# Loading weight chunks up to three ahead of their decoding, in the first batch of a fused attention, convolution-gate and token-mixing kernel

## The chip, the core and the metric

The kernel runs on one core of one Trainium2 chip. The metric is the device time of one execution in microseconds (us). Engines are named as in the profile: PE is TensorE (PEld its weight loads), DVE is VectorE, ACT is ScalarE, POOL is GpSimd, SP is SyncE. SP does nothing here but issue all transfers from one queue, in one order.

## The reference, cut to what matters

```python
# attention with 4 sink keys and a window of 128, batch 2, 8 heads, 768 tokens, head size 64
scores = scale * (q @ k.T);  scores = where(is_sink | in_window, scores, -1e9)
a = exp(scores - max);  a = a / (sum(a) + 1e-9);  x = a @ v          # -> [2, 768, 512]
# gate: w_in [512, 1024], conv_w [3, 1024], w_out [1024, 512]
h = relu(x @ w_in);  c = depthwise conv of h over 3 tokens;  x = (h * sigmoid(c)) @ w_out
# token mixing
theta = x @ w_theta;  y = w_tok_r @ (x * cos(theta)) + w_tok_i @ (x * sin(theta))
u = x + y;  out = u + relu(u @ w_ch)
```

The weights arrive as 64-bit floats.

## The kernel before, in words

A matmul of the gate is three matmuls: each operand is held as a high and a low part (`mm3`, L122 to L124). Since a weight arrives as 64-bit words, it is read in chunks of 128 rows by 512 words (512 KB) into one of six slots of 4 KB per partition and **decoded** there: ACT scales the high words (L98), DVE does three integer steps (L99 to L101), ACT writes the high part (L80), DVE the low part (L82), and the slot is free again. `w_in` and `w_out` are sixteen such chunks, numbered 0 to 15: 0 to 3 are the first half of `w_in`, 4 to 7 the first half of `w_out`, 8 to 11 and 12 to 15 the second halves. Chunks 0 and 1 are loaded ahead of everything, in before and after alike.

Attention runs in four **units** (two batches, two halves of three query tiles), each of four head **pairs**. A pair loads q and k (L261, L262) into one of three buffers, makes scores on PE (L272), their maximum on DVE (L288), the exponential on ACT (L292), sums and reciprocals on DVE (L295, L296), and normalised probabilities split into two fp16 parts by ACT (L314) and DVE (L315) in a buffer `pb`, which SP transposes by DMA into `pt` (L322). The first four heads are transposed by PE instead (L339 to L343). The values of a pair of a batch are read into a slot (L198), scaled and split by ACT and DVE into a second slot (L203 to L210), and transposed by DMA into `vp` (L212). PE forms the sink rows from `vp` (L235) and multiplies `pt` by `vp` (L380); ACT and DVE store the result as `xg` (L400, L401). So **weights and values draw on the same six slots**, taken in the order of a free list.

The gate runs in blocks: scores of the hidden layer from all four pairs' `xg` (L122 to L124 into `ps_h`), relu and convolution on ACT and DVE (L597 to L606), then L616 to L622. The sixteen blocks of the first four groups of 256 tokens are written between the pairs of the units; after each pair of unit n the code also decodes CHUNKS[n][p] chunks: 1, 1, 3, 6 in the first unit, 2, 2, 0, 1 in the second. The remaining blocks, the rotations and the token mixing follow after the attention.

What an engine does in which order is not what the code's order says: a list scheduler reorders each engine's instructions and SP's transfers when the program is built. Moving an allocation in the code therefore moves the slots that later loads get, their dependences, and through them the order on every engine.

Before the change a chunk's load is written at the place where it is decoded in the first batch; only in the third unit, where no chunk is left, stands a 1.

Of the kernel before, what the change touches and what calls it, by code (L numbers as in the profile page):

```python
# [50 lines left out]
DEC2 = 3  # L51
SA = 2
EARLY = 1
W_AHEAD = (0, 0, 1, 0)
BIG = 8.0e9
SP = 4096.0
TWO_PI = 2.0 * math.pi
# [485 lines left out]
def weight_load(tc, c, i):  # L543

    n, i = divmod(i, 8)
    if i < CC:
        src = c.w_in[i * P : (i + 1) * P, 2 * n * DM : 2 * (n + 1) * DM]
    else:
        src = c.w_out[(4 * n + i - CC) * P : (4 * n + i - CC + 1) * P, :]
    raw, slot = c.raw.tile([P, DM, 2], I32)  # L550
    tc.nc.sync.dma_start(raw.rearrange("p n w -> p (n w)"), src)
    return raw, slot
# [171 lines left out]
def body(tc, c, general):  # L724
# [49 lines left out]
    for n, unit in enumerate(units):  # L774
        unit.start()
        for p in range(4):
            unit.pair(p)
            for _ in range(CHUNKS[n][p]):
                next(weights)
                while len(c.wraw) < W_AHEAD[n] and c.nw + len(c.wraw) < 16:  # L780
                    c.wraw.append(weight_load(tc, c, c.nw + len(c.wraw)))
# [167 lines left out]
```

## Time and profile before

| what | us |
|---|---|
| median of 3 runs | 461.32 |
| the runs | 460.97, 461.32, 463.22 |
| the profiled execution, whole | 463.23 |
| its span, first to last instruction | 461.4 |
| PE busy in the span | 413.2 (90%) |
| DVE busy | 334.2 (72%) |
| ACT busy | 291.5 (63%) |
| POOL busy | 35.5 (8%) |

The span is what the rows of a trace add up to; 1.8 us of the execution lie around it. Busy shares are means over stages with different limits, so the windows of the span, not the totals, tell which engine is full at what time. The bracket behind a row of a timeline is the time that the engine stood idle just before that instruction and the instruction or transfer that ended it.

### The profile page before, as it was taken

How to read it: one execution, taken by the hardware profiler on the slowest of the kernel's cores; microseconds unless marked ns; L12 is line 12 of the kernel's file. 1: busy time of each engine (PE TensorE's matmuls, PEld its weight loads, DVE VectorE, ACT ScalarE, POOL GpSimd, SP SyncE). 2: the span in 40 equal slices, each digit the busy share in tenths (PEclk: the TensorE clock that was granted, in tenths of full speed). 3: DMA queues.
4: the chain of work that ended last, by engine and by line, in shares of the span. 5: the costliest groups of instructions: out<-in, count | busy, mean ns of one | idle time of the engine just before them, and what ended most of it. 6: DMA issues, size and time to landing. Idle time of an engine off the chain costs nothing.

```text
span 461.4 us, 7204 instructions
## 1 busy us (share of the span) xinstructions
PE 413.2 (90%) x2376; PEld 334.9 (73%) x2376; DVE 334.2 (72%) x898; ACT 291.5 (63%) x717; POOL 35.5 (8%) x120
## 2 busy tenths in 40 slices
PE   1587739699889999999999999899979999999995
PEld 0465528587677887988888887688858888888874
DVE  3879989999889886865699877995599963211132
ACT  2799878978899886875685778875675431100010
POOL 4001210031221110110000000000000000000000
PEclk9989867899999999999999999999999999999999
DMA  6786999459888442212435200230037620000012
GB/s 180 208 230 148 248 247 293 107 117 201 181 169 166 103 92 48 47 38 39 139 88 164 70 1 0 70 92 23 0 93 223 195 84 23 24 23 24 23 45 75
DMA packets 73245, 50.07 MB, mean 109 GB/s; under 512 B 59376, under 2 KB 62448, under 8 KB 73200
## 3 DMA queue, kind: packets, MB, share of 16 engines
q1 hardware_dynamic: 73200, 49.54, 42.6%
q8 instruction: 20, 0.33, 0.3%
q14 instruction: 25, 0.20, 0.1%
HBM read 32.09 MB, written 3.15 MB: 76 GB/s over the span
## 4 chain that ended last, share of the span: by engine, by line
PE 67%; DVE 16%; DMA 8%; ACT 4%; issue 3%; SPq 1%; POOL 0%; DVEq 0%; ACTq 0%; POOLq 0%
PE ps_y L123 7%; PE ps_y L124 7%; PE ps_y L122 7%; PE ps_x L616 5%; PE ps_s L272 5%; PE ps_x L617 4%; PE ps_m L122 4%; PE ps_x L622 4%; PE ps_m L124 4%; PE ps_m L123 4%; PE ps_o L380 4%; PE ps_h L122 4%; PE ps_h L124 3%; PE ps_h L123 3%; DMA pt<-pb 3%
## 5 line engine op out<-in xcount | busy, mean ns | idle before, releaser
L272 PE MATMUL ps_s<-qk 128*128 128x260 f32 (+1 forms) x192 | 60.4, 420 | 20.4 <-DVE mx L288 11.1
L122 PE MATMUL ps_y<-z_hi,wt_hi 128*128 128x512 f32 x144 | 57.7, 401 | 1.6 <-ACT z_hi L80 1.6
L122 PE MATMUL ps_h<-xg_hi,win_hi 128*128 128x258 f32 x192 | 58.6, 307 | 0.4 <-ACT h L597 0.4
L124 PE MATMUL ps_y<-z_lo,wt_hi 128*128 128x512 f32 x144 | 56.7, 397 | 0.4 <-DVE z_lo L82 0.4
L123 PE MATMUL ps_y<-z_hi,wt_lo 128*128 128x512 f32 x144 | 56.9, 395 | 0.0
L124 PE MATMUL ps_h<-xg_lo,win_hi 128*128 128x258 f32 x192 | 56.0, 296 | 0.4 <-DVE xg_lo L401 0.3
L272 PEld LDWEIGHTS ps_s<-qk 128*128 128x128 f32 x192 | 34.2, 211 | 29.5 <-DVE mx L288 15.6
L123 PE MATMUL ps_h<-xg_hi,win_lo 128*128 128x258 f32 x192 | 55.4, 290 | 0.0
L80 ACT ACTIVATE xt_hi<-ps_t 128x512 fp32r<-128x512 f32 x24 | 14.0, 594 | 61.1 <-PE ps_t L650 61.0
L292 ACT ACTIVATE e<-e,mx 128x260 f32<-128x260 f32 (+1 forms) x96 | 47.3, 496 | 7.2 <-DVE mx L288 6.9
L601 DVE SCALAR_TENSOR_TENSOR cv<-h,cw_t,cv 128x256 f32<-128x256 f32 x96 | 44.8, 478 | 6.8 <-ACT cv L599 6.1
L288 DVE CUSTOM_DVE_ANT_0 e<-ps_s,m 128x260 f32<-128x260 f32 (+1 forms) x96 | 37.7, 399 | 10.4 <-PE ps_s L272 9.0
L616 PE MATMUL ps_x<-wout_hi,ghi 128*128 128x512 f32 x96 | 40.9, 426 | 3.4 <-ACT ghi L80 3.4
L718 DVE SCALAR_TENSOR_TENSOR slot<-ps_m,slot 128x512 f32<-128x512 f32 x12 | 8.3, 691 | 44.1 <-PE ps_m L124 44.1
L122 PEld LDWEIGHTS ps_h<-xg_hi,win_hi 128*128 128x128 f32 x192 | 36.8, 192 | 3.7 <-ACT h L597 1.2
L617 PE MATMUL ps_x<-wout_lo,ghi 128*128 128x512 f32 x96 | 38.7, 403 | 0.0
L124 PEld LDWEIGHTS ps_h<-xg_lo,win_hi 128*128 128x128 f32 x192 | 36.8, 193 | 1.9 <-issue 0.5
L123 PEld LDWEIGHTS ps_h<-xg_hi,win_lo 128*128 128x128 f32 x192 | 36.9, 192 | 1.4
L314 ACT ACTIVATE pb<-e,ri 128x256 f16<-128x256 f32 (+1 forms) x84 | 35.4, 494 | 1.9 <-DVE ri L296 1.2
L315 DVE SCALAR_TENSOR_TENSOR pb<-e,ri,pb 128x256 f16<-128x256 f32 (+1 forms) x84 | 35.5, 459 | 1.2 <-ACT pb L314 1.1
L380 PE MATMUL ps_o<-pt,vp 128*64 128x256 f16 (+2 forms) x348 | 23.8, 261 | 11.8 <-DMA pt<-pb 5.4
L380 PEld LDWEIGHTS <-vp 128*64 128x64 f16 (+1 forms) x348 | 17.9, 113 | 22.5 <-issue 13.3
(134 smaller groups left out, 927.6 us busy)
## 6 DMA issues: line engine op xcount, KB each, us to landing
raw<-in_w_tok_r_dram SPq DMA_DIRECT2D x12, 384.0 KB, 3.3
raw<-in_w_tok_i_dram SPq DMA_DIRECT2D x12, 384.0 KB, 3.5
slot<-in_w_in_dram SPq DMA_DIRECT2D x8, 512.0 KB, 6.1
slot<-in_w_out_dram SPq DMA_DIRECT2D x8, 512.0 KB, 4.7
qk<-in_q_dram SPq DMA_DIRECT2D x32, 96.0 KB, 3.3
slot<-in_vt_dram SPq DMA_DIRECT2D x8, 384.0 KB, 3.7
out_dram<-slot SPq DMA_DIRECT2D x12, 256.0 KB, 2.0
qk<-in_k_dram SPq DMA_DIRECT2D x8, 262.0 KB, 3.2
```

The lines of the kernel that those rows point to most:

```text
L122: nc.tensor.matmul(out, whi, xhi, start=first, stop=False)
L123: nc.tensor.matmul(out, wlo, xhi, start=False, stop=False)
L124: nc.tensor.matmul(out, whi, xlo, start=False, stop=last)
L272: nc.tensor.matmul(ps[:, :n], qk[0][:, a, i * P : (i + 1) * P], qk[1][:, o : o + n], start=True, stop=True)
L288: nc.vector.tensor_tensor_reduce(out=e[:, i, :n], in0=ps[:, :n], in1=m, scale=-1.0 / math.sqrt(D), scalar=3.0e38, op0=ALU.add, op1=ALU.min ...
L292: nc.scalar.activation(e[:, i, :n], e[:, i, :n], AF.Exp, bias=mx[:, i : i + 1], scale=-1.0, accum_out=sm[:, i : i + 1])
L314: nc.scalar.activation(hi, src, AF.Copy, scale=r)
L315: nc.vector.scalar_tensor_tensor(lo, src, r, hi, ALU.mult, ALU.subtract)
L380: nc.tensor.matmul(po[a * D : (a + 1) * D, q], w[:, a * D : (a + 1) * D], pts[a][: w.shape[0], b0:b1, :], start=(n == 0), stop=(n == len(j ...
L601: nc.vector.scalar_tensor_tensor(cv[:, n, :], h[:, n, k : GT + k], w[:, k : k + 1], cv[:, n, :], ALU.mult, ALU.add)
L616: nc.tensor.matmul(self.px[t], ghi[:, n, s], whi, start=f2 == 0 and n == 0, stop=False)
L617: nc.tensor.matmul(self.px[t], ghi[:, n, s], wlo, start=False, stop=False)
```

## The change

`W_AHEAD[n]` is how many loaded but not yet decoded chunks the code tries to keep in unit n. After each decoded chunk the loop at L780 issues loads until that many wait. It goes from 0 to 3 in both units of the first batch.

```diff
-W_AHEAD = (0, 0, 1, 0)
+W_AHEAD = (3, 3, 1, 0)
```

No instruction is added or removed on any engine. What moves is the order. On SP's queue, at the start of the first unit, there stood before (`qk` are q and k, `vt` the values that L198 loads, `vp` their transposed parts, the numbers name buffers):

```order
L198 DMA slot3_103<-in_vt_dram 128x768
L261 DMA qk2_197<-in_q_dram 64x384 x2
L262 DMA qk2_197<-in_k_dram 128x392
L198 DMA slot5_105<-in_vt_dram 128x768
L551 DMA slot0_100<-in_w_in_dram 128x1024
L261 DMA qk0_107<-in_q_dram 64x384
L198 DMA slot1_101<-in_vt_dram 128x768
L261 DMA qk0_107<-in_q_dram 64x384
L262 DMA qk0_107<-in_k_dram 128x392
L212 DMA_TRANSPOSE vp_305<-slot4_104 128x12x128
L198 DMA slot3_103<-in_vt_dram 128x768
```

and now:

```order
L198 DMA slot3_103<-in_vt_dram 128x768
L551 DMA slot5_105<-in_w_in_dram 128x1024
L261 DMA qk2_197<-in_q_dram 64x384
L551 DMA slot2_102<-in_w_in_dram 128x1024
L261 DMA qk2_197<-in_q_dram 64x384
L262 DMA qk2_197<-in_k_dram 128x392
L551 DMA slot0_100<-in_w_out_dram 128x1024
L261 DMA qk0_107<-in_q_dram 64x384
L551 DMA slot1_101<-in_w_out_dram 128x1024
L261 DMA qk0_107<-in_q_dram 64x384
L262 DMA qk0_107<-in_k_dram 128x392
L212 DMA_TRANSPOSE vp_305<-slot4_104 128x12x128
L198 DMA slot3_103<-in_vt_dram 128x768
```

Four weight loads (chunks 2 to 5) now stand in front of the first transpose of values, where one stood; the values of the second and third pair, which had been loaded ahead of it into slots 5 and 1, are now loaded one after the other into slot 3, each after the pair before has been split.

On ACT, in the same stretch, before:

```order
L292 ACTIVATE e_226,sm_228<-e_226,mx_227 128x260
L209 ACTIVATE slot4_104<-slot3_103,vst_297 128x768
L292 ACTIVATE e_261,sm_263<-e_261,mx_262 128x128
L203 ACTIVATE slot2_102,vst_429<-slot5_105 128x768
L292 ACTIVATE e_261,sm_263<-e_261,mx_262 128x260
L333 ACTIVATE h_244<-ident_76,ri_229 128x128 x3
L98 ACTIVATE dec_t_568<-slot0_100 128x512
L292 ACTIVATE e_261,sm_263<-e_261,mx_262 128x260
L292 ACTIVATE e_329,sm_331<-e_329,mx_330 128x128
L209 ACTIVATE slot2_102<-slot5_105,vst_429 128x768
```

and now:

```order
L292 ACTIVATE e_226,sm_228<-e_226,mx_227 128x260
L98 ACTIVATE dec_t_570<-slot5_105 128x512
L209 ACTIVATE slot4_104<-slot3_103,vst_297 128x768
L292 ACTIVATE e_261,sm_263<-e_261,mx_262 128x128
L292 ACTIVATE e_261,sm_263<-e_261,mx_262 128x260
L333 ACTIVATE h_244<-ident_76,ri_229 128x128 x3
L98 ACTIVATE dec_t_578<-slot2_102 128x512
L292 ACTIVATE e_261,sm_263<-e_261,mx_262 128x260
L292 ACTIVATE e_331,sm_333<-e_331,mx_332 128x128
L98 ACTIVATE dec_t_586<-slot0_100 128x512
```

The decoding of chunks has moved up, and the second pair's values (L203, L209) have moved down.

## Rows read from the trace of the kernel before

**Rows 1.** windows of the span: busy us (and instructions) of each engine, clock, DMA share, GB/s

```profile
core 0: us, PE busy (x) PEld busy (x) DVE busy (x) ACT busy (x) POOL busy (x), PEclk, DMA share, GB/s
20.00:40.00 20.00, 16.49 (x113) 13.21 (x114) 15.22 (x63) 19.62 (x63) 0.61 (x3) 0.91 0.88 213
40.00:50.00 10.00, 6.27 (x51) 4.26 (x49) 10.00 (x34) 8.88 (x26) 2.62 (x6) 1.00 0.60 140
50.00:75.00 25.00, 16.39 (x84) 11.34 (x85) 22.66 (x72) 19.70 (x56) 3.50 (x14) 0.66 1.10 277
75.00:100.00 25.00, 21.35 (x154) 17.69 (x154) 25.00 (x72) 21.66 (x58) 3.62 (x8) 0.86 0.55 141
100.00:150.00 50.00, 46.09 (x342) 36.84 (x340) 44.72 (x169) 46.93 (x145) 11.06 (x33) 1.00 0.87 179
150.00:220.00 70.00, 70.00 (x499) 58.67 (x495) 50.20 (x145) 51.81 (x134) 8.08 (x26) 1.00 0.31 61
220.00:280.00 60.00, 59.73 (x362) 52.94 (x362) 50.87 (x108) 44.10 (x95) 0.00 (x0) 1.00 0.30 89
280.00:340.00 60.00, 56.61 (x261) 44.74 (x260) 47.14 (x78) 44.67 (x80) 0.00 (x0) 1.00 0.12 36
```

**Rows 2.** ACT in order of time: start, duration, instruction, [idle before it, releaser]

```profile
42.96 0.66 ACT L98 ACTIVATE dec_t<-slot 128x512 f32<-128x512 f32 x1 [1.11 <-DMA slot<-in_w_out_dram]
64.13 1.24 ACT L98 ACTIVATE dec_t<-slot 128x512 f32<-128x512 f32 x2 [2.55 <-DMA slot<-in_w_in_dram]
```

**Rows 3.** DVE in order of time

```profile
55.04 0.48 DVE L401 SCALAR_TENSOR_TENSOR xg_lo<-ps_o,vst,xg_hi 128x257 fp32r<-128x257 f32 x1 [0.52 <-ACT xg_hi L400]
64.82 1.00 DVE L99 TENSOR_SCALAR slot<-slot 128x512 int32<-128x512 int32 x2 [1.32 <-ACT dec_t L98]
```

**Rows 4.** the chain that ended last, from 36 to 75 us: start, duration, what

```profile
55.96 8.15 DMA slot<-in_w_in_dram
```

**Rows 5.** groups by line and shape: busy us, mean ns, idle before

```profile
L98 ACT ACTIVATE dec_t<-slot 128x512 f32<-128x512 f32 x16 | 10.6, 668 | 9.4 <-DMA slot<-in_w_in_dram 7.8 <-DMA slot<-in_w_out_dram 1.1 <-DVE cw L99 0.5
L101 DVE SCALAR_TENSOR_TENSOR slot<-slot 128x512 int32<-128x512 int32 x16 | 11.0, 687 | 0.0
L203 ACT ACTIVATE slot<-slot 128x768 f32<-128x768 f32 x8 | 6.7, 838 | 0.4 <-DMA slot<-in_vt_dram 0.4
L209 ACT ACTIVATE slot<-slot,vst 128x768 f16<-128x768 f32 x8 | 7.5, 931 | 0.0
L210 DVE SCALAR_TENSOR_TENSOR slot<-slot,vst,slot 128x768 f16<-128x768 f32 x8 | 8.1, 1010 | 0.1
```

**Rows 6.** SP's queue in order of time

```profile
15.93 0.33 SPq L551 DMA_DIRECT2D slot<-in_w_in_dram  x1
25.59 1.43 SPq L212 DMA_TRANSPOSE vp<-slot  x1
60.32 6.98 SPq L322 DMA_TRANSPOSE pt<-pb  x2
```

**Rows 7.** DMA issues between 9 and 32 us: KB each, median us to landing

```profile
slot<-in_vt_dram SPq DMA_DIRECT2D x4, 384.0 KB, 4.1
vp<-slot SPq DMA_TRANSPOSE x2, 4.1
```

**Rows 8.** DMA issues between 48 and 72 us

```profile
slot<-in_w_in_dram SPq DMA_DIRECT2D x4, 512.0 KB, 7.5
pt<-pb SPq DMA_TRANSPOSE x5, 6.0
```

**Rows 9.** PE in order of time

```profile
25.02 0.49 PE L235 MATMUL ps_o<-vp,sink_rows 128*36 128x128 f16 x6 [1.77 <-DMA vp<-slot]
68.31 1.76 PE L380 MATMUL ps_o<-pt,vp 128*64 128x256 f16 x17 [2.95 <-DMA pt<-pb]
```

## The prediction, made before the changed kernel ran

> **What bounds the kernel now.** I read the windows of the span first, because the totals mix stages. In [rows 1] look for the engine that is busy for the whole of a window. From 20 to 40 us that is ACT (19.62 of 20), and DVE, which waits on it, has 4.78 us idle. From 40 to 100 us it is DVE: 10.00 of 10, then 22.66 of 25, then 25.00 of 25. From 100 to 150 us ACT (46.93) and PE (46.09 of 50) are both close to full. From 150 us on it is PE: 70.00 of 70, then 59.73 of 60. So the end is set by PE's work, which the change leaves alone, plus the time for which PE stood idle before 150 us. A microsecond gained early reaches the end if DVE and ACT pass it on until PE takes over; nothing after 150 us swallows it, because PE has no gap there that could close or open.
>
> Then I read who waited for weights. The loads that the change moves end three waits of ACT for `w_in` and `w_out`: in the group of L98 7.8 and 1.1 us [rows 5], of which the first (5.3 us, for chunk 0, loaded at the start in both kernels) stays. What is left is 1.11 us at 42.96 and 2.55 us at 64.13 [rows 2]. Only the second reaches DVE, as 1.32 us at 64.82 [rows 3]; the chain of waits shows the same place as one transfer of 8.15 us from 55.96 [rows 4]. There SP had issued six weight loads almost at once, and the transposes of probabilities behind them suffered too: two of them took 6.98 us to issue [rows 6], their median landing was 6.0 us [rows 8], and PE waited 2.95 us for one [rows 9].
>
> **The change part by part.** No instruction appears or goes; the terms are waits.
>
> (a) Weight waits between 50 and 75 us. In the new order chunks 2 to 5 are loaded before about 20 us, and behind them the burst is cut up: of the six loads that stood in a row, each pair now has a transpose between. DVE's idle time there is 2.34 us (25 - 22.66) [rows 1], of which 1.32 us is the weight's own [rows 3]; 0.52 us of the rest waits for a pair's output [rows 3], which the transposes held up. I take 1.8, between 1.3 and 2.3.
>
> (b) ACT's full stretch from 20 to 40 us. Two of the values' instructions leave it net: L203 and L209 of the third pair and L203 of the fourth go (0.838 + 0.931 + 0.838 = 2.6 us), L203 of the second pair and L98 of chunk 5 come (0.838 + 0.668 = 1.5 us) [rows 5]. ACT is 1.1 us lighter. DVE gets about 2 us more work there (the steps of chunks 4 and 5 at 0.69 each, less one L210 of 1.01 [rows 5]) and has 4.78 us of room [rows 1], so that work is hidden; if the room were gone, it would cost its 2 us at once. Gain 1.1, between 0 and 2.2 (the work that DVE can take in).
>
> (c) A new wait: values. The second pair's `vt` load now stands behind the first transpose of values. ACT's L209 of the second pair is its 47th instruction (it was the 21st), that of the third pair the 77th (it was the 39th). ACT reached its 47th at 35 us and its 77th at 49 us in the trace. Splitting on DVE takes 1.01 us [rows 5], issuing the transpose 1.43 [rows 6] and landing 4.1 from the issue on [rows 7], so `vp` is there at about 40.5 and 55 us. Queued behind it on PE are the sink rows (L235) and behind these the next scores, and DVE waits for the scores. In the new order they are wanted at about 40 and 54.5 us. SP, which waits for each split, has the next q and k and the next weights behind it; those are wanted later. That PE can be held in this way the trace shows at the first pair, 1.77 us before L235 [rows 9]. Cost 0.7, between 0 and 2.0.
>
> The front is worth 1.8 + 1.1 - 0.7 = 2.2 us.
>
> (d) The stage from 100 to 150 us. PE is idle there for 3.91 us (50 - 46.09) while ACT is full [rows 1]. In the new order the scheduler puts the second group's blocks ahead of later attention: the relu (L597) of the eighth block is ACT's 271st instruction instead of the 285th, and the tanh (L605) of the fifth the 233rd instead of the 244th. Fourteen places at ACT's 46.93 us for 145 instructions [rows 1], 0.32 us each, are 4.5 us of ACT work that no longer stands before PE's matmuls. That cannot give more than the 3.91 us of idle; I take 1.8, the middle, between 0 and 3.9. Against it stands the first block, whose tanh moves from the 139th to the 150th place; its cover is that PE has attention matmuls to do meanwhile and is not the bound before 100 us.
>
> (e) The tail. Between 220 and 340 us the order of blocks and rotations also differs; PE is idle 3.39 us from 280 to 340 [rows 1]. No row says which way that moves: 0, between -1.5 and +1.5.
>
> Sum: 2.2 + 1.8 = 4.0 us off. The profiled execution's own time of 463.23 (span 461.4) would become 459.2. It was 1.9 us above the median of the three runs, 461.32; taken from the median, the forecast is 457.3 us.
>
> **The rivals.** First, forecast: the waits go and the new ones are small. For it speaks that DVE's idle time of 50 to 75 us hangs on one row with a weight as releaser. Time 457.3, between 453.5 and 459.
>
> Second, the change does less than it says. There are six slots, and from chunk 6 on nothing is loaded further ahead: the decoding of chunk 6 moves from ACT's 86th place to the 100th, of chunk 15 from the 144th to the 163rd. Then the wait on weights has only been exchanged for the wait on values (a, b and c cancel), the first blocks come later, and a part of (d), 0.8 us, is left: 460.5. Against it: ACT had no gap for values in the trace, 0.4 us in all for L203 [rows 5].
>
> Third, slower: values that arrive late one after another. One link from pair to pair is now issue of the transpose 1.43 [rows 6], load of `vt` 4.1 [rows 7], L203 0.84, L209 0.93, L210 1.01 [rows 5]: 8.3 us. The order leaves 30 ACT instructions between the second pair's L209 and the third's, with the reads of the exponentials' sums some 39 in the profile's count, at 19.62 us for 63 [rows 1] 12.1 us. So there are 3.8 us of slack, and it decides from a `vt` landing of 7.9 us on. 512 KB loads took a median of 7.5 in the crowded stretch [rows 8], and one 8.15 [rows 4]; now 2 MB of weights are loaded where one chunk (15.93) was [rows 6]. Every later microsecond stops PE's scores and so DVE. If the transposes for the second and third pair land 4 us later than I reckon, 1.5 + 4.5 = 6 us are lost and (d) is lost too: 461.3 - 2.9 + 6 = 464.4. Against it: the median for `vt` was 4.1 where the transfers were already 0.88 busy [rows 1, 7]. The Trainium skill bears on this rival in "DMA: Bandwidth & Descriptors", section "Queues, rings and completion order": on each transfer engine the descriptors are consumed in ring order, so a small urgent load cannot pass a large early one on the same queue. By that rule the early weights are paid for by q, k and values; whether they are in use at that moment the trace of before does not show, since it has few weights there.
>
> **How the numbers follow.** About 0.5% (2.3 us) is what a measurement of this kernel can tell from no change, so faster means under 459.0 and slower over 463.6. Forecast 0.53; second rival 0.27, all of it within the band; third 0.20, of which 0.17 is slower and 0.03 within. A part of the forecast's spread, through (e), lies in the band too: 0.01. So faster 0.52, same 0.31, slower 0.17. The range takes in the forecast's bounds (all of a to e at their best: 461.3 - 2.3 - 2.2 - 3.9 - 1.5 = 451.4; that they all come together I leave out) and the third rival's price: 453.5 to 464.5.
>
> **What would show it.** In the trace after: no idle time of ACT before L98 with a weight as releaser after 20 us (a); DVE's idle from 50 to 75 us under 1 us (a); ACT still full and DVE busier than 15.22 us from 20 to 40 us (b); PE's wait before L235 on `vp` under 2 us for the second and third pair, and L203 without an idle time over 1 us (c); PE's idle from 100 to 150 us near 2 us (d); PE's idle from 280 to 340 us between 2 and 5 us (e). I am wrong if L203 or L235 wait for values by several microseconds, or if DVE's idle time merely moves from 64 us to another place.

## The result, and the profile after

The changed kernel takes 465.89 us (median of six runs, 464.62 to 466.58) where the kernel before takes 461.37: the ratio is 1.0084, with a 95% interval of 1.0059 to 1.0109. It is 4.5 us slower, where 4 us less was forecast. Its profiled execution took 466.22 us with a span of 464.4 us. Three kernels below had one much slower execution each (e1_queue 479.88 us, e2_slots42 810.69, e8_queue_before 482.50), which their medians count and the ratios leave out.

The windows of the span after the change (busy us and instructions of each engine, clock, DMA share, GB/s), to be read beside [rows 1]:

```profile
core 0: us, PE busy (x) PEld busy (x) DVE busy (x) ACT busy (x) POOL busy (x), PEclk, DMA share, GB/s
20.00:40.00 20.00, 16.14 (x111) 12.32 (x112) 18.47 (x70) 19.85 (x67) 0.60 (x3) 1.00 0.69 169
40.00:50.00 10.00, 7.01 (x53) 4.83 (x52) 8.21 (x34) 8.84 (x24) 1.95 (x9) 1.00 0.86 202
50.00:75.00 25.00, 15.38 (x88) 10.29 (x89) 21.22 (x74) 23.24 (x67) 4.38 (x12) 0.75 1.16 243
75.00:100.00 25.00, 21.29 (x145) 16.98 (x145) 22.61 (x63) 18.45 (x49) 3.88 (x10) 0.84 0.87 209
100.00:150.00 50.00, 43.74 (x306) 35.85 (x306) 42.16 (x145) 42.54 (x120) 7.69 (x25) 0.90 0.68 139
150.00:220.00 70.00, 70.00 (x502) 59.55 (x501) 54.34 (x167) 55.91 (x152) 10.20 (x32) 1.00 0.39 77
220.00:280.00 60.00, 60.00 (x372) 52.39 (x371) 49.10 (x105) 42.05 (x89) 0.00 (x0) 1.00 0.29 88
280.00:340.00 60.00, 58.31 (x279) 47.53 (x278) 48.15 (x78) 44.39 (x82) 0.00 (x0) 1.00 0.11 36
```

DVE is where to look up to 100 us. From 20 to 40 us it does more than before (18.47 instead of 15.22). From 40 to 100 us, where it had 2.34 us idle in all, it now has 7.96 (60 less 8.21, 21.22 and 22.61). From 100 to 150 us PE's idle time has grown from 3.91 to 6.26 us, at a lower clock (0.90). The lower clock is that of 115 to 130 us, from PE's longest wait on: 0.72, 0.50 and 0.76 in steps of 5 us, where the kernel before has 1.00 throughout. From 280 to 340 us PE's idle time has fallen, from 3.39 to 1.69.

What DVE and PE wait for now, on PE in order of time (in brackets the idle time and what ended it):

```profile
40.37 0.49 PE L235 MATMUL ps_o<-vp,sink_rows 128*36 128x128 f16 x6 [1.11 <-DMA vp<-slot]
56.85 0.61 PE L235 MATMUL ps_o<-vp,sink_rows 128*36 128x128 f16 x4 [3.15 <-DMA vp<-slot]
74.14 0.32 PE L380 MATMUL ps_o<-pt,vp 128*64 128x128 f16 x2 [3.88 <-DMA pt<-pb]
87.11 1.15 PE L380 MATMUL ps_o<-pt,vp 128*64 128x128 f16 x23 [2.38 <-DMA pt<-pb]
119.00 2.08 PE L380 MATMUL ps_o<-pt,vp 128*64 128x128 f16 x23 [4.44 <-DMA pt<-pb]
```

and on DVE:

```profile
41.54 0.43 DVE L288 CUSTOM_DVE_ANT_0 e<-ps_s,m 128x260 f32<-128x260 f32 x1 [1.14 <-PE ps_s L272]
60.48 0.43 DVE L288 CUSTOM_DVE_ANT_0 e<-ps_s,m 128x260 f32<-128x260 f32 x1 [2.40 <-PE ps_s L272]
```

Each of DVE's two waits for scores follows one of PE's waits for values: the scores stand behind the sink rows. Between 20 and 130 us the weights are gone as a cause: of 1.11 and 2.55 us [rows 2] 0.34 is left on ACT, which waits for values instead:

```profile
42.29 0.84 ACT L203 ACTIVATE slot<-slot 128x768 f32<-128x768 f32 x1 [0.90 <-DMA slot<-in_vt_dram]
62.45 0.67 ACT L98 ACTIVATE dec_t<-slot 128x512 f32<-128x512 f32 x1 [0.34 <-DMA slot<-in_w_out_dram]
117.46 0.84 ACT L203 ACTIVATE slot<-slot 128x768 f32<-128x768 f32 x1 [3.01 <-DMA slot<-in_vt_dram]
```

The chain of waits of the changed kernel (start, duration, what) has five long transfers between 38 and 119 us, none of them a weight:

```profile
38.12 4.08 DMA slot<-in_vt_dram
...
51.17 5.64 DMA vp<-slot
...
66.11 7.98 DMA pt<-pb
...
80.84 6.24 DMA pt<-pb
...
113.82 5.15 DMA pt<-pb
```

SP's queue shows the order behind them. Transposes of values are issued at 21.65, 36.35 and 51.17 us. The second pair's `vt` load goes out right behind the first of them, the third pair's right behind the second, and the fourth pair's at 44.55; before, the first three transposes stood at 20.54, 25.59 and 34.58.

```profile
21.65 1.94 SPq L212 DMA_TRANSPOSE vp<-slot  x1
23.65 0.64 SPq L198 DMA_DIRECT2D slot<-in_vt_dram  x1
36.35 1.72 SPq L212 DMA_TRANSPOSE vp<-slot  x1
38.12 0.78 SPq L198 DMA_DIRECT2D slot<-in_vt_dram  x1
...
44.55 0.33 SPq L198 DMA_DIRECT2D slot<-in_vt_dram  x1
...
51.17 1.64 SPq L212 DMA_TRANSPOSE vp<-slot  x1
...
65.19 0.34 SPq L551 DMA_DIRECT2D slot<-in_w_in_dram  x1
66.11 2.96 SPq L322 DMA_TRANSPOSE pt<-pb  x1
...
91.38 0.33 SPq L198 DMA_DIRECT2D slot<-in_vt_dram  x1
```

and in the kernel before:

```profile
20.54 1.94 SPq L212 DMA_TRANSPOSE vp<-slot  x1
...
34.58 1.44 SPq L212 DMA_TRANSPOSE vp<-slot  x1
...
75.67 0.38 SPq L551 DMA_DIRECT2D slot<-in_w_out_dram  x1
...
81.73 0.54 SPq L198 DMA_DIRECT2D slot<-in_vt_dram  x1
```

Weights that are held ahead take up to four of the six slots, so the first three pairs of values use the same two slots in turn: the next `vt` load goes out only behind the transposes of the pair before, which wait for that pair's split. Later it is weights that wait: the load at 65.19 goes out late, into a slot that values' transposes held, and the `pt` transpose of 66.11 right behind it takes 7.98 us to land. The second batch's first `vt` load is at 91.38 us instead of 81.73. It stands behind the last weight load, which goes out at 89.58 us instead of 75.67; the last weight chunk is decoded at ACT's 163rd place instead of the 144th.

### The profile page after: what moved, and what is told of

The parts are those of the page before. It is cut to its first block, busy times and chain, and to the rows that moved or that the text cites. A ratio compares the mean times of both kernels' runs of the same rounds, so it can differ in the third digit from the quotient of the medians.

```text
span 464.4 us, 7200 instructions
## 1 busy us (share of the span) xinstructions
PE 414.6 (89%) x2376; PEld 336.4 (72%) x2376; DVE 335.6 (72%) x898; ACT 292.3 (63%) x717; POOL 34.7 (7%) x120
## 3 DMA queue, kind: packets, MB, share of 16 engines
HBM read 32.09 MB, written 3.15 MB: 76 GB/s over the span
## 4 chain that ended last, share of the span: by engine, by line
PE 77%; DVE 9%; DMA 9%; issue 1%; ACT 1%; SPq 1%; DVEq 0%; ACTq 0%
PE ps_s L272 7%; PE ps_y L123 7%; PE ps_y L124 7%; PE ps_y L122 7%; PE ps_o L380 5%; PE ps_m L122 5%; PE ps_x L616 5%; PE ps_m L124 5%; PE ps_x L617 5%; PE ps_m L123 5%; PE ps_x L622 4%; PE ps_h L124 4%; PE ps_h L122 4%; DMA pt<-pb 4%; PE ps_h L123 4%; DMA vp<-slot 2%
## 5 line engine op out<-in xcount | busy, mean ns | idle before, releaser
L272 PE MATMUL ps_s<-qk 128*128 128x260 f32 (+1 forms) x192 | 61.5, 429 | 20.2 <-DVE mx L288 10.9
L124 PE MATMUL ps_h<-xg_lo,win_hi 128*128 128x258 f32 x192 | 55.5, 294 | 0.7 <-DVE xg_lo L401 0.7
L292 ACT ACTIVATE e<-e,mx 128x260 f32<-128x260 f32 (+1 forms) x96 | 46.5, 486 | 10.7 <-DVE mx L288 10.1
L380 PE MATMUL ps_o<-pt,vp 128*64 128x256 f16 (+2 forms) x348 | 25.7, 275 | 12.4 <-DMA pt<-pb 12.3
L380 PEld LDWEIGHTS <-vp 128*64 128x64 f16 (+1 forms) x348 | 19.5, 120 | 20.7 <-issue 16.0
```

Source lines behind the costliest of these rows:

```text
L124: nc.tensor.matmul(out, whi, xlo, start=False, stop=last)
L272: nc.tensor.matmul(ps[:, :n], qk[0][:, a, i * P : (i + 1) * P], qk[1][:, o : o + n], start=True, stop=True)
L292: nc.scalar.activation(e[:, i, :n], e[:, i, :n], AF.Exp, bias=mx[:, i : i + 1], scale=-1.0, accum_out=sm[:, i : i + 1])
L380: nc.tensor.matmul(po[a * D : (a + 1) * D, q], w[:, a * D : (a + 1) * D], pts[a][: w.shape[0], b0:b1, :], start=(n == 0), stop=(n == len(j ...
```

## The experiments

Every edit here moves instructions on all engines, so one time does not say where it was won or lost. I therefore work out a **lost time** for each kernel: the end of an instruction less the sum of the work of its engine up to there, each kind of instruction taken at its median duration in the trace of the kernel before. It holds waiting and slower clock alike. Matmuls overlap, so of each only the part that the one before does not cover is counted; how that is reckoned moves PE's first column by about the same amount in every row, so that only differences between rows are read from it. Columns: median of the runs, ratio to runs of the kernel before beside it (their medians lay from 461.4 to 462.1); PE's lost time by 145 us of its work (attention nearly done), between 145 and 200, and from 200 us of work to the last matmul; DVE's lost time between 24 and 48 us of its work, where the first batch's values come in.

```
kernel               median  ratio     PE 0-145  145-200  200-end   DVE 24-48
before               461.37  1           55.7      2.0      7.6        0.4
e14_unit2_only       462.09  1.0001      55.2      1.4      7.5        1.0
after                465.89  1.0084      61.1      1.1      5.7        7.1
e13_unit1_only       464.98  1.0055      60.4      1.2      5.8        7.0
e1_queue             472.44  1.0226      59.3      1.1     11.2        6.7
e2_slots42           474.10  1.0224      62.4      4.9      8.7        6.4
e3_slots33           484.81  1.0516      69.8      1.2     14.8        5.5
e4_ahead1            468.45  1.0148      59.1      1.1     10.3        2.2
e5_vtin_after        466.01  1.0089      55.7      0.9     10.9        1.2
e6_vtin_before       470.20  1.0148      61.9      1.5      7.6        3.1
e7_vtin_queue        492.36  1.0657      78.3      4.4     12.8       16.4
e8_queue_before      477.06  1.0313      68.5      1.2      7.3        3.5
e9_second_batch      465.69  1.0088      58.0      1.4      7.6        7.1
e10_first_batch      467.91  1.0148      57.0      0.5     10.9        0.9
e11_second_before    462.91  1.0026      55.4      1.6      7.5        0.1
e12_slots42_before   472.14  1.0248      58.8      4.3     10.4        4.7
e15_vtin_ahead1      473.15  1.0258      57.1      5.0     12.8        1.4
e16_vtin_ahead2      468.49  1.0152      58.4      0.6     10.9        1.2
e17_rotate_a         460.05  0.9963      59.0      0.9      4.4        2.5
e18_rotate_b         462.39  1.0019      57.8      0.8      6.6        3.1
```

Three theories stood at the start, and their letters stand in the expectations. V: values are chained through two slots. Q: transposes of probabilities stand on SP behind weight loads that wait for a slot. O: the chunks 6 to 15 are decoded later, and what follows them with them.

**Where the change acts.** Each unit's setting alone:

```diff
-W_AHEAD = (3, 3, 1, 0)
+W_AHEAD = (3, 0, 1, 0)
```

> W_AHEAD = (3, 0, 1, 0): loading ahead in the first unit alone. The order on every engine is that of the changed kernel word for word. If all of the change comes from the first unit, 464.5 to 467, and PE's accumulated idle time at the end of attention 60 to 62 us as there; if the second unit's setting costs something that the order doesn't show, 461 to 464.

```diff
-W_AHEAD = (3, 3, 1, 0)
+W_AHEAD = (0, 3, 1, 0)
```

> W_AHEAD = (0, 3, 1, 0): loading ahead in the second unit alone. The order is that of the kernel before on every engine, but for one weight load that stands ahead of a load of k instead of behind it. 460.5 to 463. Its profile is a second one of practically the kernel before: if PE's accumulated idle time is 1 to 2 us lower than in the first from 40 us on, the difference between profile and median of the kernel before lay in the first stages.

The first takes 464.98 us (ratio 1.0055, 1.0024 to 1.0085), the second 462.09 (1.0001, 0.9975 to 1.0027). The second unit's setting does nothing; the first unit's is the change. These two also profile both orders once more, and the pairs agree: by 145 us of work PE has lost 55.7 and 55.2 us in the old order, 61.1 and 60.4 in the new, and from 200 us on 7.6 and 7.5 against 5.7 and 5.8. So the new order loses 5.3 us up to the end of attention, and the tail gives 1.8 back. Most of the 5.3 us arises late: at 55 us of PE's work (111 us of time) the new order has lost 0.7 and 2.0 us more than the old, at 60 us of work (127 us of time) 10.0 and 10.4, at 80 us of work 4.9 and 4.7. The lower loss that I had looked for in the second profile of the old order, 1 to 2 us from the first stages on, is there in part: 0.5 us by 145, 1.2 by the end.

**Weight loads on another queue**, in the changed kernel and in the kernel before:

```diff
-    tc.nc.sync.dma_start(raw.rearrange("p n w -> p (n w)"), src)
+    tc.nc.gpsimd.dma_start(raw.rearrange("p n w -> p (n w)"), src)
     return raw, slot
```

> The changed kernel with weight_load issued by POOL's queue instead of SP's; the order on ACT stays within a few places of the changed kernel's (values' L209 at places 11, 44, 82, 87 instead of 12, 47, 77, 90; last weight chunk 153 instead of 158). Theory V (chained values: the loss is PE held at the sink rows L235 and what follows): the waits at L235 stay (1.5, 1.1, 3.2 us), time 464 to 467. Theory Q (SP's queue: transposes of probabilities stand behind weight loads that wait for a slot, 3.88 and 2.38 us before L380): these two waits fall under 1 us, time 459 to 462.5. Theory O (the order: chunks 6 to 15 are decoded 14 to 20 places later on ACT, so the first blocks come later): nothing of that changes, 464 to 467, with both kinds of wait free to move.

> The kernel before with weight loads issued by POOL's queue: control for the run with the changed kernel on that queue (472.4). If the queue itself costs what made that run slow, this is 468 to 474 too, with DVE behind by 1 us at the start and PE's idle time from 220 to 340 us up by 3 us or more; if the loads ahead are at fault, it is 459 to 463.

472.44 and 477.06 us: all three theories missed the first, and the control shows why it says little. Loads that wait for a slot hold whatever is behind them, on POOL as on SP, and on POOL these are the sink columns of the probabilities, without which no `pt` transpose starts. POOL of the kernel before with this edit:

```profile
54.89 0.53 POOL L551 DMA_DIRECT2D slot<-in_w_in_dram  x1 [6.98 <-DMA vp<-slot]
55.41 1.04 POOL L551 DMA_DIRECT2D slot<-in_w_out_dram  x2
56.44 0.53 POOL L551 DMA_DIRECT2D slot<-in_w_in_dram  x1
56.99 0.21 POOL L308 TENSOR_TENSOR sk<-e,ri 128x4 f32<-128x4 f32 x1
```

L308 runs as soon as the loads are through, without an idle time of its own. What the first one does show is that the waits before L235 stay (1.37 and 3.01 us) when the weights have left SP, as V has it. Q is not settled by these runs. For one of the two transposes that Q is about, the chain of the changed kernel speaks against it: what came last before the transpose of 66.11 us was DVE (66.02), not SP. There the transfer was long, not the wait in SP's queue.

**The slots divided**, four for weights and two for values, in the changed kernel and in the kernel before, and three and three in the kernel before:

```diff
         c.raw = Slots(c.const, B * NG)
+        c.vraw = Slots(c.const, 0)
+        c.vslots, c.raw.free = c.raw.free[4:], c.raw.free[:4]
...
-    raw, slot0 = c.raw.tile([P, S], F32)
+    raw, slot0 = c.vraw.tile([P, S], F32)
...
-    parts, slot1 = c.raw.tile([P, 2, S], F16)
+    parts, slot1 = c.vraw.tile([P, 2, S], F16)
```

Left out above: values give their slots back to their own list, later the gate's output `x2` takes a slot from either list, and the run with three and three has 3 where the lines above have 4.

> The changed kernel with the six slots divided: four for weights, two for values. Values are chained as before on the changed kernel (L209 at places 12, 47, 77, 110 of ACT), but no weight load waits for a value's transposes, and the chunks 6 to 15 are decoded at 81 to 136 instead of 100 to 158. Theory V: still slow, 464 to 468, with the wait at L235 of the third and fourth pair at 3 us or more. Theory Q: the transposes of probabilities no longer land late, L380 waits under 1 us in 66 to 90 us, 459 to 462.5. Theory O: the chunks stand where the kernel before has them (86 to 138), 459 to 462.5; it differs from Q only by what PE does from 100 to 150 us (idle back under 4.5 us).

> The kernel before (W_AHEAD 0 in both units) with the six slots divided, four for weights and two for values. Nothing is loaded ahead on request, but weights no longer wait for values' slots, so SP loads chunks 2 to 5 before 20 us all the same, and values are chained through their two slots (L209 at places 11, 46, 79, 109 of ACT). If the chain of values is what costs, whoever makes it, this is as slow as the changed kernel with divided slots (470 to 476). If the request to load ahead costs something by itself, this lies at 460 to 464.

> The kernel before (nothing loaded ahead on request) with the six slots divided three and three. Values are not chained (L203 at places 7, 18, 36, 52 of ACT, L209 at 11, 29, 43, 63), but chunks 6 to 15 are decoded at 81 to 172, later than in the changed kernel. Theory V: no loss at L235 (under 1 us from the second pair on), time 458 to 462. Theory Q: weight loads wait only for a decoding, but these are late, so transposes behind them may be late: 461 to 466. Theory O: the latest chunks of all, so the slowest of all, 466 to 470, with PE's idle time from 100 to 150 us over 6 us.

474.1, 472.14 and 484.81 us. The pair with two slots for values is the cleanest answer on V, though the first is slower than V's 464 to 468: whether loading ahead is asked for or not, the kernel is about 10 and 11 us slower than before (ratios 1.0224 and 1.0248), and DVE loses 6.4 and 4.7 us where the kernel before loses 0.4. In the kernel before with this edit the transposes of values are issued 16 to 17 us apart, as they were 15 apart after the change, and PE waits for them:

```profile
20.21 2.33 SPq L212 DMA_TRANSPOSE vp<-slot  x1
...
36.84 1.91 SPq L212 DMA_TRANSPOSE vp<-slot  x1
...
54.11 1.92 SPq L212 DMA_TRANSPOSE vp<-slot  x1
...
70.46 3.06 SPq L212 DMA_TRANSPOSE vp<-slot  x1
```

```profile
58.59 0.61 PE L235 MATMUL ps_o<-vp,sink_rows 128*36 128x128 f16 x4 [3.58 <-DMA vp<-slot]
```

In this run the wait reaches DVE by another way: ACT's copy of the sink rows (L239, at 59.45) waits 3.22 us for PE, and DVE waits 1.73 us for the exponential behind it.

With three and three, values are free (no wait before L235 over 1 us), but the weights are starved: the last weight chunk is decoded at ACT's 176th place, PE waits 2.70, 3.36 and 3.64 us for `pt`, and from 100 to 150 us it is idle for 7.19 us:

```profile
100.00:150.00 50.00, 42.81 (x293) 35.65 (x291) 41.89 (x144) 42.51 (x119) 7.53 (x25) 0.93 0.73 157
```

That is what O forecast, the slowest of all four of that comparison with over 6 us idle, though the time went beyond its 470. V's forecast for this run fails: values are not all that six slots decide. DVE loses 5.5 us here too, in the column where the values come in; its longest idle time there is 1.46 us, for the decoding of a weight chunk. So that column by itself does not tell what was waited for.

**One chunk ahead instead of three:**

```diff
-W_AHEAD = (3, 3, 1, 0)
+W_AHEAD = (1, 1, 1, 0)
```

> The changed kernel with W_AHEAD = (1, 1, 1, 0): one chunk is held ahead instead of three. Values' L209 at places 11, 20, 44, 79 of ACT, chunks 6 to 15 at 49 to 136 (before 63 to 138). Theory V: the second pair's values are as early as before, 459 to 462, L235 waits under 1.5 us at the second pair. Theory Q: the loads from 45 to 60 us still stand in a row of two to four before transposes, 460 to 463. Theory O: chunks as early as before or earlier, 458 to 461.5.

468.45 us, outside all three forecasts. No wait before L235 over 1 us, as V said (DVE loses 2.2 us there). But a transpose of probabilities goes out at 49.51 us behind four weight loads (45.70 to 48.74), and in the chain of waits it takes 9.04 us; PE waits for it 6.22 us, longer than for any `pt` in the two kernels' first traces (though e14_unit2_only, in the old order, has a wait of 5.40 at 62.19):

```profile
49.51 9.04 DMA pt<-pb
```

```profile
58.60 1.76 PE L380 MATMUL ps_o<-pt,vp 128*64 128x256 f16 x17 [6.22 <-DMA pt<-pb]
```

**Values with one slot instead of two.** `vt` is loaded into the `vp` tile, which has the same size and is written by the transposes only when `vt` has been read:

```diff
-    raw, slot0 = c.raw.tile([P, S], F32)
+    v = c.vp.tile([P, 2 * NT, P], F16, name="vp")
+    raw = v.rearrange("p a k -> p (a k)").bitcast(F32)
...
-    v = c.vp.tile([P, 2 * NT, P], F16, name="vp")
...
-    c.raw.free += [slot0, slot1]
+    c.raw.free.append(slot1)
```

In the changed kernel, in the kernel before, and in the changed kernel with the weights on POOL's queue too:

> The changed kernel with vt loaded into the vp tile that its transposes write later, so that a pair of values takes one slot instead of two and no vt load waits for a slot; nothing else changes. The first transposes of the second and third pair then stand right behind each other on SP, and chunks 6 to 15 stand at 60 to 138 of ACT instead of 100 to 158. Theory V (the loss is the chain of values through the slots and what it delays): L235 waits under 1 us after the first pair, PE's accumulated idle time at the end of attention back to that of the kernel before (56 us instead of 61), 458 to 462. Theory Q (transposes of probabilities behind weight loads on SP): three or four weight loads still stand in a row before them, so L380's waits for pt stay at 5 us or more in sum and the time at 463 to 467.

> The same edit in the kernel before (nothing loaded ahead on request): control for the run above. Theory V: values were not chained there, so little changes, 459 to 463, and the run above lies within 2 us of it. Theory Q: loads stand in rows of four before the transposes as in the kernel before; 460 to 464, and the run above is 2 us or more slower, by the loads ahead.

> The changed kernel with both edits: vt into the vp tile, and weight loads issued by POOL's queue. Theory V alone: as the kernel with vt in the vp tile, plus the 1 us by which a start on POOL's queue was later (461 to 464). Theory Q alone: as the kernel with the loads on POOL's queue, 470 to 474. Both together: neither wait is left, 455 to 460.

466.01, 470.2 and 492.36 us. The last is outside every forecast; I take it for POOL's queue again, which was not followed up. In the first the chain is gone: the transposes of the second and third pair stand right behind each other on SP,

```profile
30.94 4.88 SPq L212 DMA_TRANSPOSE vp<-slot  x2
```

DVE loses 1.2 us where it lost 7.1, and PE has lost 55.7 us by 145, as in the kernel before: V's stage forecast (56) holds. Two waits before L235 stay, though (1.45 and 2.35 us, the second for the fourth pair), and V's time fails, since the tail now loses 10.9 us instead of 5.7. Q's time (463 to 467) holds, but PE's waits for a `pt` before L380, 2.08, 0.73 and 1.57 us, are below its 5 us in sum. The control is outside both forecasts (459 to 464) and 4.2 us slower than the first by the medians (PE has lost 61.9 us by 145), though one of its four executions, 464.18 us, is faster than all of the first's. With one slot for a pair of values, three chunks ahead are better than none in three executions of four, the other way round than with two slots; why none is so slow there stays open.

The same edit for one batch alone (`if b == 1` or `if b == 0` ahead of the new lines), with a control:

> The changed kernel with vt loaded into the vp tile for the second batch alone. Up to the 58th DMA of SP the order is that of the changed kernel word for word, so the first batch's chain and its waits stay (L235 1.1 and 3.2 us, L380 3.9 and 2.4 us); what goes is that the second batch's vt loads wait for slots that late weight chunks hold. Theory V1 (the loss that stays comes from the first batch's chain, 40 to 90 us): PE's accumulated idle time at the end of attention stays near 61 us, time 464 to 467. Theory V2 (the first batch's loss is made up again, and what decides is the second batch's values behind the late chunks, 110 to 130 us): 56 to 57 us, time 459.5 to 462.5.

> The complement: vt into the vp tile for the first batch alone. The first batch's values take one slot each, chunks 6 to 15 are decoded at 60 to 138 of ACT instead of 100 to 158, the second batch's values need slots as before. Theory V1: PE's accumulated idle time at the end of attention 56 us, time as with the edit in both batches or better, 461 to 466. Theory V2: since the second batch's slots now come free earlier too (chunk 15 at 138), a part of the gain comes here as well: 462 to 465, with the second batch's vt loads issued back at 82 to 110 us.

> The kernel before with the edit in the second batch alone: control for the changed kernel with that edit. V1: nothing waits there in the kernel before, so 460 to 463. V2: the same, 460 to 463, and the changed kernel with this edit within 1.5 us of it.

465.69, 467.91 and 462.91 us. Up to 145 us of work the second batch's half brings 2.8 us (58.0 against 60.8, the mean of 60.4 and 61.1), the first batch's 3.8 (57.0). These are one profile each, and fronts of one order differ by up to 3.3 us (below); the second batch's half rests better on the window from 100 to 150 us, where PE is idle for 6.26 and 6.15 us in the two profiles of the new order and for 3.54 with this edit. So both theories on the batch seem half right: the loss has two places, the first batch's values and, 60 us later, the second batch's. The times don't follow: that of the second run is above both forecasts, and the tails lose 7.6 and 10.9 us after 200 us of work.

One and two chunks ahead with this edit:

> vt loaded into the vp tile, W_AHEAD = (1, 1, 1, 0). If loading ahead gains by itself where values take one slot, the time lies between that of none ahead (470.2) and of three (466.0): 466 to 470. If those two differ only by the luck of their orders, it lies anywhere from 461 to 474, outside these bounds as likely as inside.

> The same with W_AHEAD = (2, 2, 1, 0). By the trend: 465 to 468, below one ahead. By luck: anywhere from 461 to 474.

473.15 and 468.49 us: none, one, two and three ahead give 470.2, 473.2, 468.5 and 466.0. Three ahead is the best of the four, but one is worse than none: the sign holds for three against none, a trend it is not.

**The tail by itself.** The changed kernel with `vt` in the `vp` tile, and only the places of the rotations moved:

```diff
-ROTATE = (1, 2, 0, 0, 0, 1, 0, 2)
+ROTATE = (1, 2, 0, 0, 1, 0, 0, 2)
```

> The changed kernel with vt in the vp tile and ROTATE = (1, 2, 0, 0, 1, 0, 0, 2): the fourth rotation stands one block earlier. If the loss after 200 us of PE work is the order's alone, this tail, more like that of the changed kernel, loses 6 to 9 us instead of 10.9, and the time is 461 to 464.5, while PE's accumulated idle time at the end of attention stays at 55.5 to 57 us. If the late loss is the early gain given back to something that the order doesn't set, 465 to 467 again.

> The same with ROTATE = (0, 3, 0, 0, 0, 1, 0, 2): the first rotation stands behind the second block. By the order alone: the tail loses another amount than 10.9, 6 to 12, and the time moves with it by the same amount, 461 to 467, with attention's end unchanged. If given back otherwise: 465 to 467.

460.05 us (ratio 0.9963, 0.9939 to 0.9987) and 462.39 (1.0019, 1.0000 to 1.0038): 6.0 and 3.6 us less than without the move. The tail loses 4.4 and 6.6 us instead of 10.9. The first run lies below its forecasts (461 to 464.5 us, a tail of 6 to 9), and by 145 us of work both have lost more than the 55.5 to 57 us that I had named. The window of the tail without the move:

```profile
280.00:340.00 60.00, 55.12 (x247) 43.81 (x245) 45.35 (x78) 41.74 (x77) 0.00 (x0) 0.97 0.11 36
```

and with the first move:

```profile
280.00:340.00 60.00, 58.85 (x273) 46.87 (x271) 49.28 (x85) 44.22 (x82) 0.00 (x0) 1.00 0.12 36
```

So the late loss comes with the order: the two profiles of each order above agree to 0.1 us in the tail, and a move of the rotations alone takes 4.3 to 6.5 us off it. What PE waits for there was not traced. The kernel with the first move is the only one here that is below the kernel before, by 1.5 us; neither the kernel before nor the changed kernel was run with the same move, so how much of it is due to the loads ahead stays open. Up to 145 us of work these two lost 59.0 and 57.8 us, with the order that lost 55.7 before and differs from theirs only from 230 us on (the first one's profiled execution, 462.20 us, is 2.15 above its median): the front of one order differs by up to 3.3 us from execution to execution. With that spread, values off the slots bring back about 3 of the 5.3 us (57.4, the mean of the four runs that have the first batch's off, against 60.8), and in no run did loading ahead bring PE's loss by 145 us below that of the kernel before.

## Why the prediction was wrong, step by step

(a) **Weight waits, forecast 1.8 us gained: right.** ACT's waits for weights are gone. In DVE's lost time the place is the stretch from 48 to 56 us of its work: 2.2 and 2.0 us in the two profiles of the old order, 0 in both of the new. But the check that I gave, DVE under 1 us idle from 50 to 75 us, fails with 3.78 (25 - 21.22): the idle time has come back under another name, which I had listed as the sign of being wrong.

(b) **ACT lighter, forecast 1.1 us gained: right in kind.** By 24 us of work DVE has lost 9.9 us instead of 14.4, and in the second profiles of the two orders 12.5 instead of 13.1: a gain of 4.5 and of 0.6 us, so the size is not settled. In that second profile of the new order the clock from 20 to 40 us was 0.83, and DVE waited 2.78 us for PE.

(c) **Wait for values, forecast 0.7 us lost, at most 2.0: the first step that failed.** The first wait was nearly as worked out: `vp` was forecast for 40.5 us and came at 40.4, and PE stood at the sink rows at 39.3 (the starts above less the idle times) instead of 40. The second was not. `vp` came at 56.85 us instead of 55, 1.85 late, of which its landing is 1.5 (5.64 us instead of the 4.1 that I took from [rows 7]); PE stood there at 53.7 instead of 54.5. Told from the first release on, PE was back at the sink rows after 13.3 us where I had 14, and the values came after 16.5 us where I had 14.5. The second profile of the new order repeats it, 13.1 and 16.6 us:

```profile
43.20 0.65 PE L235 MATMUL ps_o<-vp,sink_rows 128*36 128x128 f16 x6 [1.29 <-DMA vp<-slot]
59.83 0.61 PE L235 MATMUL ps_o<-vp,sink_rows 128*36 128x128 f16 x4 [3.52 <-DMA vp<-slot]
```

There the gain of (b) was only 0.6 us and PE came 2.6 us later than in the first profile, yet it waited as long. So it was the step from one pair of values to the next that was too long for PE, not PE that came early by the gains. And I priced the two waits of PE alone, 4.26 us by the trace (1.11 + 3.15), where each also holds the scores, DVE's next pair, the split of the next values behind that, and the weight loads that wait for the slots. DVE's loss between 24 and 48 us of its work is 7.1 and 7.0 us in the new order and 0.4 and 1.0 in the old: 6.3 us, not 0.7. The two kernels with two slots for values (4.7 and 6.4) and those with the first batch's `vt` in the `vp` tile (0.9 to 3.1, but for the one on POOL's queue) show that it is the chain that costs this; only the kernel with three slots for each kind loses as much (5.5) without it, to other waits. With what (a) and (b) gain, DVE has by 56 us of its work lost 17.0 us as in the kernel before, in the second profiles 19.5 against 16.1. So the front as a whole, forecast as 2.2 us gained, is 0.7 and 2.0 us lost where PE has done 55 us of its work.

The third rival had this mechanism and almost this price (6 us), but the wrong condition. I let it decide from a `vt` landing of 7.9 us on; `vt` landed in 4.08 us and the rival came all the same. Its link, 8.3 us, took the steps of values back to back. In the trace a link is 14.8 us (51.17 - 36.35): the split's two halves on ACT, L203 at 42.29 and L209 at 48.34, stand 6 us apart, behind other work in ACT's and DVE's order. That is 2.7 us more than the 12.1 us that I had as a link's due, without any slow transfer. The Trainium skill's rule that I had put beside it ("DMA: Bandwidth & Descriptors", section "Queues, rings and completion order") was not needed for `vt`. The same passage of the Trainium skill says that a later write may finish before an earlier one, so that "cannot pass" went further than it does. With the order of the rings the trace is in keeping at the transposes of probabilities: the one issued 0.9 us behind a 512 KB weight load took 7.98 us, and those issued at 46.23 and 48.73 us, with no weight load on its way, 3.6 each. Whether ring order or shared bandwidth did that, no run here told apart.

(d) **The stage from 100 to 150 us, forecast 1.8 us gained: wrong in sign, the second step that failed and by PE's loss the larger.** From 55 to 145 us of its work PE loses 4.5 and 3.1 us more than in the old order. PE's idle time grew by 2.35 us (6.26 - 3.91), in the second profiles by 1.62 (6.15 - 4.53). I had followed the blocks that move ahead, and not the slots: the chunks 6 to 15 come later, the second batch's `vt` loads wait for their slots (91.38 instead of 81.73 us), ACT waits 3.01 us before L203, PE 4.44 us for a `pt`. Nor had I a term for the clock. Between 55 and 60 us of its work PE loses 10.1 us (9.2 in the second profile; 0.8 in both of the old order), of which 5.7 is idle time and the rest slower work: the 23 matmuls of L380 take 2.08 us at 119.00 and 1.15 at 87.11 (both above), and the granted clock from 120 to 125 us is 0.50, in both profiles. With the second batch's `vt` off the slots PE's loss falls by 2.8 us (that between 55 and 60 us of work to 6.8), and the window's idle time to 3.54 us:

```profile
100.00:150.00 50.00, 46.46 (x327) 38.61 (x322) 43.46 (x152) 43.13 (x126) 6.15 (x26) 0.93 0.73 143
```

(e) **The tail, forecast 0, between -1.5 and +1.5: mis-sized.** It gave 1.8 us back. That the order alone can move it by 6.5 us (4.4 to 10.9 from one front) I had not allowed for; the range that I gave it was too narrow, and my sign for it fails as well (PE idle for 1.69 us from 280 to 340, where I had named 2 to 5).

The sum by stages, over the two profiles of each order: 5.3 us lost up to the end of attention (0.7 and 2.0 by 55 us of PE's work, the rest behind it), 0.6 gained from 145 to 200, 1.8 gained in the tail, 2.9 us in all. The spans of these profiles differ by 3.3 us on average, and the medians of the two programs in this order lie 2.9 and 4.5 us above the kernel before. How much of that is due to values waiting for slots the times do not show, since every kernel without these waits has another tail as well; by PE's loss it is about 3 of the 5.3 us, and the other 2 stay open. Of what the prediction said on the bound, the first half held: PE's work and what it loses before 150 us set most of the end. That nothing after 150 us moves it did not hold.

The second rival (waits exchanged, no change) came nearest in the front: by DVE's 56 us of work (a), (b) and (c) cancel in the first profiles, though not in the second (19.5 against 16.1). It fails at (d), of which it kept a gain of 0.8 us.

## What to carry to other kernels

Loading ahead is paid for with the buffers that it holds: before judging it, write down for each buffer of the ring who has it now and who takes it next, also for the tiles that only share the ring (here values and, one batch later, values again). Price a chain of buffer, split, transfer and buffer by its length in the trace, with the other work that stands in its engines' queues between the steps, not by the sum of its own steps. Price a wait of PE with what the clock does behind it: here 5.7 us of idle time cost about 10. And where a scheduler reorders the program, compare kernels stage by stage: seven of these eighteen lost over 3 us more than the kernel before in a tail whose work is the same in all of them.

## What the hardware showed beyond that

The same order from the start ran with another clock in two executions. The changed kernel's first profile has a granted clock of 1.00 from 20 to 40 us; the second profile of that order has

```profile
20.00:40.00 20.00, 17.18 (x106) 13.08 (x107) 15.76 (x59) 17.46 (x57) 0.59 (x3) 0.83 0.56 140
```

Taken in steps of 5 us it is 1.00 there but for 0.63 from 25 to 30 us and 0.68 from 30 to 35, a mix of the two levels (1.2 and 2.4 GHz, 0.5 and 1.00 here). At its start PE stood idle for 1.61 us (up to 26.87, waiting for the first pair's values); in the first profile it stood idle there for 1.49 us, and the clock did not fall. With the lower clock ACT is busy for 17.46 us instead of 19.85 and DVE for 15.76 instead of 18.47, and DVE waits 2.78 us for PE where its longest such wait was 0.72. By 145 us of work the two are only 0.7 us apart again, and it is the one with the lower clock that has lost less.
